# Attention and MLP on one Trainium2 core: transposing k and q on VectorE in 32 by 32 blocks, from block loads on two queues

## The chip, the cores and the metric

The kernel runs on 1 core of one Trainium2 chip. The metric is the device time of one execution in microseconds (us). Four compute engines appear below by short names: PE (TensorE, with its weight loads shown apart as PEld), DVE (VectorE), ACT (ScalarE) and POOL (GpSimd). SP (SyncE) does no arithmetic and issues DMAs; ACT can issue them too. In the profile, SPq and ACTq are the instruction queues of those engines when they issue a DMA.

## The reference

A decayed linear attention over 4 batches, 8 heads, 768 tokens and head size 64, in blocks of 64 tokens, followed by a two-layer MLP on the 3072 x 512 result. Everything is float32.

```python
for b in range(nb):
    sl = slice(b * block, (b + 1) * block)
    qb, kb, vb = (q[:, :, sl], k[:, :, sl], v[:, :, sl])
    intra = np.einsum('bhic,bhjc->bhij', qb, kb) * Dmask[None]
    intra = np.einsum('bhij,bhjd->bhid', intra, vb)
    inter = np.einsum('bhid,bhde->bhie', qb * lam_pow[None], kv_state)
    out[:, :, sl] = intra + inter
    kb_dec = kb * rev_pow[None]
    kv_state = lam_block[None, :, None, None] * kv_state + np.einsum('bhsd,bhse->bhde', kb_dec, vb)
...
h = x @ w_in                      # x: attention output, (3072, 512); w_in: (512, 2048)
g = np.maximum(0.01 * h, h)
return (g @ w_out).astype(np.float32)
```

`Dmask`, `lam_pow`, `rev_pow` and `lam_block` are powers of one factor per head.

## The kernel before

**Tiling.** Tokens come in 24 chunks of 128 (two blocks of 64), six per batch. Four chunks make a group of 512 tokens, so there are six groups. The inner layer is cut into 8 pieces `p` of 256 columns. Each operand of the MLP is kept as three arrays `h`, `l` and `m` (a high part, a scaled rest and a combination), and each product is the sum of three matmul passes over them: `h` and `l` first, then an ACT pass over the PSUM bank (L579), then `m`, and a second ACT pass with the leaky ReLU (L582).

**Stages.** `alone(c)` and `begun(c)` do the first chunks. `round_of(c)` is one attention round: it finishes chunk `c` (`outputs`), forms the scores of chunk `c + 1` (`scores`) and transposes k and q of chunk `c + 2` (`transposes`), and it loads k, q and v of chunk `c + 2`. `up(g, p)` is one up-projection step of a group, 48 matmuls of 512 columns for a whole group (L561), and writes the 512 KB result `G` to DRAM (L585). From group 2 on, every second up step has a round beside it: rounds 12 to 23 stand beside the up steps of groups 2 to 4. When all groups are through, `down_load` and `down` read `G` back and do the second layer (L620) to the end. `w_in(p)` and `w_out(p)` turn the weights, which arrive as 64-bit words, into float32 (three ACT passes, L497 to L501, and two DVE passes, L503 and L504, per half piece); `w_out` then parks its result in DRAM (`WO`, L538), and `w_out_parts` fetches it back in group 5, where the attention buffers are free.

**Transposes.** The scores need k and q with the head dimension on the partitions. `transposes` (L319) does that with four 128 x 128 PE transposes for k into `po` (or a `b` bank for the first chunks) and four for q into `pt` (L331), and two ACT copies bring them into `kTs` and `qTs` (L340, L341). POOL then scales k (L345) and q (L349). k is also needed untransposed, for the state update (`kv`, L364).

**Loads.** `load_kq` (L304) loads k and q of a chunk with two 128 KB DMAs each, all on SP, into the double buffers `kqv[0]` and `kqv[1]`; `load_v` loads v. Rows of 64 floats make packets of 256 bytes.

**Order of the work.** [...] `Plan.add` (L61) records each operation with its engine, an assumed duration, the keys that it reads and writes and a rank; `Plan.emit` (L81) places them by a greedy list schedule and emits the instructions in that order, so every engine's queue is fixed at build time. The plan has one lane called DMA, which stands for SP's queue, and takes a DMA's result as usable 3.5 us after the lane is through with it. In a round, PE's pieces are chained so that nothing comes between them (`plan.begin`, `plan.end`). A small copy `seen_po` (L414) lets PE start the second state product (`inter(1)`, L417); it may go to DVE or ACT, as the plan finds.

**DMA completion.** In the built program all DMAs of SP and ACT share eight landing counters, handed out in turn. A DMA waits for the one that used its counter last, and its issuing engine waits with it, in order.

**Buffers.** `raw` is three buffers of 4 KB per partition for the arriving weight words, used in turn; from the down stage on the last one holds the output scratch `tt`. `gs` is two output buffers of `up`. The PSUM banks `b10`, `b11` and `b2` rotate among the blocks of `up`.

Of the kernel before, what the change touches and what calls it, by code (L numbers as in the profile page):

```python
# [36 lines left out]
class Plan:  # L37
# [23 lines left out]
    def add(self, eng, us, fn, reads=(), writes=(), rank=0.0):  # L61

        n, deps = len(self.ops), set()
        for k in reads:
            w, r = self.last.setdefault(k, [None, []])
            if w is not None:
                deps.add(w)
            r.append(n)
        for k in writes:
            w, r = self.last.setdefault(k, [None, []])  # L70
            if w is not None:
                deps.add(w)
            deps.update(r)
            self.last[k] = [n, []]
        deps.discard(n)
        ways = {eng: us} if isinstance(eng, str) else dict(zip(eng, us))
        if self.chain is not None:
            self.chains[self.chain].append(n)
        self.ops.append((ways, fn, deps, (self.rank + rank, n), set(writes)))
# [81 lines left out]
def kernel(  # L161
# [10 lines left out]
    nc = tc.nc  # L172
    P = 128
    B, H, SEQ, D = q.shape
    C, C2 = P, P // 2
    NCB = SEQ // C
    HP = H // 2
    d_model, d_ff = moe_w_in.shape
    KO = d_model // P
    NP = d_ff // (2 * P)  # L180
    NCH = B * NCB
    GC = 4
    NG = NCH // GC
    T = GC * C
# [3 lines left out]
    QS = 0  # L188
    KM = 1
    NRAW = 3  # L190
    HALF = (slice(0, D), slice(D, 2 * D))
    assert D == 64 and KO == HP == 4 and SEQ % C == 0 and NCH % GC == 0 and d_model == T == 512 and NP % 4 == 0

    pool = ctx.enter_context(tc.tile_pool(name="sb", bufs=1))
    psum = ctx.enter_context(tc.tile_pool(name="ps", bufs=1, space=bass.MemoryType.PSUM))
# [6 lines left out]
    def ps(shape, name):  # L202
        return psum.tile(shape, F32, name=name, tag=name)


    pt = ps([P, HP, C], "pt")
# [6 lines left out]
    X = [[sb([P, KO, T], f"x{x}{i}", F32R) for x in "hlm"] for i in range(2)]  # L213
    raw = [sb([P, 2 * d_model], f"raw{i}") for i in range(NRAW)]
    lows = [sb([P, d_model], f"low{i}", I32) for i in range(2)]
# [11 lines left out]
    def part(n):  # L227
        nonlocal used
        used += n
        assert used <= NA, used  # L230
        return att[:, used - n:used]

    ident = part(P)
    kqv = [[part(H * D).rearrange("p (h d) -> p h d", h=H) for _ in range(2)] for _ in range(3)]
    kTs, qTs, qsTs = ([part(HP * C).rearrange("p (y t) -> p y t", y=HP) for _ in range(2)] for _ in range(3))
    sc = part(2 * HP * C2).rearrange("p (x y t) -> p x y t", x=2, y=HP)
    state = [part(HP * D).rearrange("p (y d) -> p y d", y=HP) for _ in range(4)]
# [21 lines left out]
    add = plan.add  # L259
# [10 lines left out]
    def factors_q():  # L270
        for i in range(2):
            nc.vector.tensor_copy(lam_p[HALF[i]], lam_h[HALF[i], i::2])
        for hp in range(HP):
# [25 lines left out]
    def of(c):  # L299
        return c // NCB, c % NCB, c % 2  # L300
# [3 lines left out]
    def load_kq(c):  # L304
        b, n, i = of(c)
        for src, x, nm in ((k, 0, "k"), (q, 1, "q")):
            y, dst = src[b, :, n * C:(n + 1) * C, :], kqv[x][i]

            def go(y=y, dst=dst):
                for z in range(2):  # L310
                    nc.sync.dma_start(out=dst[:, z * HP:(z + 1) * HP, :], in_=y[z::2].rearrange("h p d -> p h d"))  # L311
            add("DMA", 1.15, go, [], [f"{nm}{i}"])

    def load_v(c):
        b, n, i = of(c)
# [3 lines left out]
    def transposes(c):  # L319
        b, n, i = of(c)  # L320
        tk, tq = kqv[0][i], kqv[1][i]
        if c < GC:
            z, key = bank[KT].rearrange("p (y t) -> p y t", y=HP), KT
            at = [z[:, y, :] for y in range(HP)]
        else:
            z, key = po[:, :, upper, :], "po"
            at = [po[:, y // 2, HP + y % 2 * 2:HP + y % 2 * 2 + 2, :].rearrange("p a t -> p (a t)") for y in range(HP)]

        def go(src, at):
            for y in range(HP):  # L330
                nc.tensor.transpose(out=at[y], in_=src[:, 2 * y:2 * y + 2, :].rearrange("p a d -> p (a d)"), identity=ident)  # L331

        add("PE", 0.44, lambda: go(tk, at), [f"k{i}"], [key])
        add("PE", 0.44, lambda: go(tq, [pt[:, y, :] for y in range(HP)]), [f"q{i}"], ["pt"])

        def copies():
            kT = kTs[i]
            into = kT if c < GC else kT.rearrange("p (t a) x -> p t (a x)", t=2)
            src = z if c < GC else z.rearrange("p t a x -> p t (a x)")
            add("ACT", 0.6, lambda: nc.scalar.copy(into, src), [key], [f"kT{i}"])  # L340
            add("ACT", 0.6, lambda: nc.scalar.copy(qTs[i], pt), ["pt"], [f"qT{i}"])  # L341
            kr = tk.rearrange("p (y x) d -> p y x d", x=2)
            nr = slice(0, C2 if n == NCB - 1 else P)
            add(*((("DVE", "POOL"), (0.7, 1.1)) if c < KM else ("POOL", 1.1)),
                lambda e="POOL": ENG[e].tensor_tensor(kr[nr], kr[nr], _bc(pow_k, 3, D)[nr], op=ALU.mult), ["fk"], [f"k{i}"])  # L345
            m = slice(1 if n == 0 else 0, 2)
            o, x = (z.rearrange("p y (t i) -> p y t i", t=2)[:, :, m, :] for z in (qsTs[i], pt if c < QS else qTs[i]))
            eng, e, us, dep = ("DVE", nc.vector, 0.7, "pt") if c < QS else ("POOL", nc.gpsimd, 1.2, f"qT{i}")
            add(eng, us, lambda: e.tensor_tensor(o, x, _bc(pow_q, 2, 2)[:, :, m, :], op=ALU.mult), ["fq", dep], [f"qsT{i}"])  # L349

        return copies
# [101 lines left out]
    def round_of(c):  # L453

        after = []
        if c + 2 < NCH:
            load_kq(c + 2)
        plan.begin(c)

        if c < 2 * GC:  # L460
            after.append(transposes(c + 2))
        after.insert(0, outputs(c, lambda: after.append(scores(c + 1)) if c + 1 < NCH else None))
        if 2 * GC <= c < NCH - 2:
            after.append(transposes(c + 2))
        plan.end()
        for x in after:
            x()
        if c + 2 < NCH:
            load_v(c + 2)

# [2 lines left out]
    n_raw = 0  # L473

    def to_float32(kind, p, h, dst, key, after=()):

        nonlocal n_raw
        j, n_raw = n_raw % len(raw), n_raw + 1
        r, low, kl = raw[j], lows[n_raw % 2], f"low{n_raw % 2}"
        d = dst.bitcast(I32)  # L480

        def load():
            r64 = r.bitcast(I64)
            if kind == "wi":
                nc.scalar.dma_start(out=r64.rearrange("p (k f) -> p k f", k=2),
                                  in_=w_in_r[:, 2 * h:2 * h + 2, p * 2 * P:(p + 1) * 2 * P])
            else:
                nc.sync.dma_start(out=r64, in_=moe_w_out[(2 * p + h) * P:(2 * p + h + 1) * P, :])

        def words(i, dt):  # L490
            return r.bitcast(dt).rearrange("p (n two) -> p n two", two=2)[:, :, i]

        def addend(dt, i):
            return low.bitcast(dt).rearrange("p (n two) -> p n two", two=2)[:, :, i]

        add("DMA", 1.6, load, after, [f"raw{j}"])
        add("ACT", 0.67, lambda: nc.scalar.activation(out=dst, in_=words(1, F32), func=AF.Abs, scale=2.0 ** -110),  # L497
            [f"raw{j}"], [key])
        add("ACT", 0.78, lambda: nc.scalar.activation(out=addend(U16, 0), in_=words(0, U32), func=AF.Copy, bias=0.0, scale=2.0 ** -29),
            [f"raw{j}"], [kl])  # L500
        add("ACT", 0.77, lambda: nc.scalar.activation(out=addend(F16, 1), in_=words(1, F32), func=AF.Copy, bias=0.0, scale=2.0 ** -100),  # L501
            [f"raw{j}"], [kl])
        add("DVE", 0.42, lambda: nc.vector.tensor_scalar(d, d, 3, None, op0=ALU.logical_shift_left), [], [key])  # L503
        add("DVE", 1.0, lambda: nc.vector.tensor_tensor(d, d, low, op=ALU.add), [kl], [key])  # L504
# [159 lines left out]
    nxt, n_out = 3 * GC, 0  # L664
    steps = [(g, p) for g in range(2, NG) for p in range(NP)]
    for n, (g, p) in enumerate(steps):
        while nxt < (g + 1) * GC:
            seq.append(("r", nxt))
            nxt += 1
        seq.append(("up", g, p))  # L670
        if nxt < NCH and nxt // GC < g + 2 and n % 2 == 0:
            seq.append(("r", nxt))
            nxt += 1
        if n_out < NP and n % 2 == 1:
            seq.append(("wo", n_out, ["G%d%d" % steps[n - 1]]))
            n_out += 1
        if g == NG - 1:
            seq.append(("wp", p))
# [5 lines left out]
    for n, x in enumerate(seq):  # L684
# [9 lines left out]
        elif x[0] == "wp":  # L694
            if not freed:
                add("DVE", 0.0, lambda: None, [], ATT + [f"gr{j}" for j in range(NR)])
                add("ACT", 0.0, lambda: None, [], [f"raw{j}" for j in range(NRAW)] + ["t0", "t1"])
                freed = True
# [37 lines left out]
```

## Time and profile before

| | |
|---|---|
| median of 3 runs | 625.87 us (625.6 to 626.18) |
| the profiled execution | 626.15 us, its span 623.6 us |
| granted TensorE clock | 1.0 throughout |
| DMA | 103706 packets, 101.51 MB, mean 163 GB/s; 78560 packets under 512 B |
| rounds 12 to 22 | one each 14 us, from 153 to 306 us |
| down stage | from 357 us to the end |

The span runs from the first instruction to the last; the execution's own time is 2.55 us more. Engine busy times are sums over the whole span; where stages differ, the tables by stage count. In the chain of waits each piece is what the next one waited for, followed back from the end. A group line gives operation, tiles, shape and count, then busy us and the mean duration in ns. The line "DMA to landing" is the time from the start of the issuing instruction to the landing of its last byte.

### The profile page before, as it was taken

How to read it: one execution, taken by the hardware profiler on the slowest of the kernel's cores; microseconds unless marked ns; L12 is line 12 of the kernel's file. 1: busy time of each engine (PE TensorE's matmuls, PEld its weight loads, DVE VectorE, ACT ScalarE, POOL GpSimd, SP SyncE). 2: the span in 40 equal slices, each digit the busy share in tenths (PEclk: the TensorE clock that was granted, in tenths of full speed). 3: DMA queues.
4: the chain of work that ended last, by engine and by line, in shares of the span. 5: the costliest groups of instructions: out<-in, count | busy, mean ns of one | idle time of the engine just before them, and what ended most of it. 6: DMA issues, size and time to landing. Idle time of an engine off the chain costs nothing.

```text
span 623.6 us, 13157 instructions
## 1 busy us (share of the span) xinstructions
PE 613.9 (98%) x5578; PEld 513.5 (82%) x5578; DVE 297.9 (48%) x366; ACT 281.2 (45%) x461; POOL 91.7 (15%) x95
## 2 busy tenths in 40 slices
PE   8899999999999999999999999999999999999997
PEld 7688888898888888888788888888888888888885
DVE  4799882400344333333145763735545454535531
ACT  3688875443577766664444722312222222314111
POOL 4852513300332222222000000000000000000000
PEclk9999999999999999999999999999999999999999
DMA  9998844632787778842455762432524333333201
GB/s 201 250 259 259 243 156 136 155 111 91 206 248 253 245 238 259 247 163 87 169 202 189 247 203 72 153 117 82 188 67 135 136 106 131 128 109 118 85 0 67
DMA packets 103706, 101.51 MB, mean 163 GB/s; under 512 B 78560, under 2 KB 80608, under 8 KB 103648
## 3 DMA queue, kind: packets, MB, share of 16 engines
q1 hardware_dynamic: 99152, 92.29, 47.3%
q10 hardware_dynamic: 4496, 8.39, 4.3%
q8 instruction: 43, 0.70, 0.5%
q14 instruction: 15, 0.12, 0.1%
HBM read 65.02 MB, written 35.65 MB: 161 GB/s over the span
## 4 chain that ended last, share of the span: by engine, by line
PE 96%; DMA 2%; SPq 0%; POOL 0%; DVE 0%; ACT 0%; issue 0%; DVEq 0%
PE b L561 43%; PE b L620 17%; PE po L620 11%; PE psc L620 10%; PE po L286 4%; PE pt L620 3%; PE psc L286 3%; PE po L331 2%; PE pt L331 2%; DMA att<-in_q_dram 2%; PE b L253 1%; DMA att<-in_k_dram 1%; SPq L311 0%; PE b L331 0%; POOL att L345 0%
## 5 line engine op out<-in xcount | busy, mean ns | idle before, releaser
L602 ACT ACTIVATE xh<-att 128x1024 fp32r<-128x1024 f32 x48 | 50.9, 1061 | 147.3 <-PE po L620 141.3
L603 DVE SCALAR_TENSOR_TENSOR xl<-att,xh 128x1024 fp32r<-128x1024 f32 x48 | 58.7, 1223 | 99.4 <-ACT xh L602 99.4
L561 PE MATMUL b<-xh,wh 128*128 128x512 f32 (+3 forms) x416 | 105.5, 377 | 0.0
L561 PE MATMUL b<-xl,wl 128*128 128x512 f32 (+3 forms) x416 | 105.4, 376 | 0.0
L561 PE MATMUL b<-xm,wm 128*128 128x512 f32 (+3 forms) x416 | 104.9, 381 | 0.0
L561 PEld LDWEIGHTS b<-xl,wl 128*128 128x128 f32 x416 | 75.5, 188 | 14.7 <-DVE wl L515 0.2
L561 PEld LDWEIGHTS b<-xh,wh 128*128 128x128 f32 x416 | 75.3, 188 | 14.3
L561 PEld LDWEIGHTS b<-xm,wm 128*128 128x128 f32 x416 | 73.5, 188 | 13.2
L579 ACT ACTIVATE b<-b 128x512 f32<-128x512 f32 (+2 forms) x98 | 56.7, 579 | 57.1 <-PE b L561 56.3
L582 ACT ACTIVATE gs<-b 128x512 f32<-128x512 f32 (+2 forms) x98 | 57.8, 590 | 48.7 <-PE b L561 40.2
L375 DVE TENSOR_TENSOR att<-psc,att 128x512 f32<-128x512 f32 x24 | 16.5, 688 | 128.3 <-PE psc L286 128.2
L620 PE MATMUL b<-wl,xl 128*128 128x512 f32 x192 | 74.7, 389 | 0.0
L620 PE MATMUL b<-wh,xh 128*128 128x512 f32 x192 | 74.7, 389 | 0.0
L605 DVE SCALAR_TENSOR_TENSOR xm<-xl,xh 128x1024 fp32r<-128x1024 f32 x48 | 58.8, 1226 | 4.8
L345 POOL TENSOR_TENSOR att<-att 128x512 f32<-128x512 f32 (+1 forms) x24 | 27.6, 1149 | 141.1 <-PE po L331 133.5
L620 PEld LDWEIGHTS b<-wh,xh 128*128 128x128 f32 x192 | 36.1, 188 | 7.5
L620 PEld LDWEIGHTS b<-wl,xl 128*128 128x128 f32 x192 | 36.0, 188 | 7.5
L385 POOL TENSOR_TENSOR att<-att 128x256 f32<-128x256 f32 x40 | 35.6, 889 | 28.7 <-DVE att L382 23.4
L620 PE MATMUL po<-wm,xm 128*128 128x512 f32 (+1 forms) x100 | 37.2, 381 | 0.7 <-ACT raw L642 0.7
L620 PE MATMUL psc<-wh,xh 128*128 128x512 f32 x96 | 37.4, 389 | 0.0
L620 PE MATMUL po<-wl,xl 128*128 128x512 f32 x96 | 37.4, 389 | 0.0
L620 PE MATMUL b<-wm,xm 128*128 128x512 f32 x96 | 37.4, 389 | 0.0
(67 smaller groups left out, 817.1 us busy)
## 6 DMA issues: line engine op xcount, KB each, us to landing
att<-g SPq DMA_DIRECT2D x48, 512.0 KB, 3.2
g<-gs SPq DMA_DIRECT2D x45, 512.0 KB, 2.9
raw<-in_moe_w_in_dram ACTq DMA_DIRECT2D x16, 512.0 KB, 5.0
raw<-in_moe_w_out_dram SPq DMA_DIRECT2D x16, 512.0 KB, 4.3
att<-in_k_dram SPq DMA_DIRECT2D x48, 128.0 KB, 4.0
att<-in_q_dram SPq DMA_DIRECT2D x48, 128.0 KB, 3.7
att<-in_v_dram SPq DMA_DIRECT2D x24, 256.0 KB, 3.9
out_dram<-gs SPq DMA_DIRECT2D x23, 256.0 KB, 2.2
```

The source lines that it names most:

```text
L286: nc.tensor.matmul(dst[HALF[cols]], lhsT=lhsT[HALF[rows]], rhs=rhs[HALF[rows]], start=start, stop=True, skip_group_check=True)
L331: nc.tensor.transpose(out=at[y], in_=src[:, 2 * y:2 * y + 2, :].rearrange("p a d -> p (a d)"), identity=ident)
L345: lambda e="POOL": ENG[e].tensor_tensor(kr[nr], kr[nr], _bc(pow_k, 3, D)[nr], op=ALU.mult), ["fk"], [f"k{i}"])
L375: add("DVE", 0.69, lambda: nc.vector.tensor_tensor(sc, psc[:, :, lower, :], decay, op=ALU.mult), ["psc", "fk"], ["sc"])
L385: add("POOL", 0.7, lambda new=new, j=j: nc.gpsimd.tensor_tensor(state[(j + 1) % 4], new, _bc(lam_c, 2, D), op=ALU.mult), [f"st{j % 4}", "f ...
L561: nc.tensor.matmul(dst, lhsT=w[z][:, kk * 2 * P + f * P:kk * 2 * P + (f + 1) * P], rhs=x[z][:, kk, toks], start=start and kk == 0, stop=kk ...
L579: add("ACT", ns, lambda b=b: nc.scalar.activation(out=b, in_=b, func=AF.Copy, bias=0.0, scale=S + 1.0), [], [kb], rank=-1.5)
L582: add("ACT", ns, lambda b=b, r=r: nc.scalar.activation(out=r, in_=b, func=AF.Prelu, bias=0.0, scale=1.0 / WS, alpha=0.01), [kb], [f"gs{jg} ...
L602: add("ACT", 1.05, lambda: nc.scalar.activation(out=h, in_=graw[j], func=AF.Copy, bias=0.0, scale=NEAR), reads, wr("h"))
L603: add("DVE", 1.25, lambda: nc.vector.scalar_tensor_tensor(l, graw[j], 1.0, h.bitcast(F32), op0=ALU.mult, op1=ALU.subtract), reads + [f"rh{ ...
L605: add("DVE", 1.25, lambda: nc.vector.scalar_tensor_tensor(m, l.bitcast(F32), -S, h.bitcast(F32), op0=ALU.mult, op1=ALU.add), [f"rh{j}", f" ...
L620: nc.tensor.matmul(acc[tb][z // 2][:, cols], lhsT=ring[j][z][:, f * T + tb * P:f * T + (tb + 1) * P], rhs=W[pp][z][:, f * d_model:(f + 1) ...
```

## The change

From chunk 12 on (`DV = 12`) k and q are no longer transposed on PE. VectorE transposes them straight into `kTs` and `qTs`, from SBUF to SBUF, with one instruction for a chunk's k and one for its q (`turn`). Such an instruction transposes each 32 x 32 block in its place and moves no block to other partitions. So the data must arrive with the blocks already where the result wants them: for each pair of chunks, `load_subs` issues 32 DMAs, 16 for k on SP and 16 for q on ACT, each with 32 partitions of 8 runs of 32 floats (32 KB, runs of 128 bytes). k's blocks go into the third `raw` buffer; q's go into the second `raw` buffer for the pair of chunks 12 and 13 and after that into the two q buffers, which are free because the plain q loads end at chunk 12. The plain k loads stay. A pair's loads are recorded in the round four before its first chunk, after the transposes of the chunk three ahead, with a rank 5 later than the rest of that round; each load has its own rank and place in the plan. An issue on ACT is entered with 0.45 us on ACT's lane.

Three things follow. `kqv` is cut from one piece per letter so that the two q buffers lie side by side. The w_out loads use only the first two `raw` buffers. And a w_out piece is converted every third up step instead of every second, so that the last one falls on step 22 rather than on step 15 (of 32).

In the built program TensorE has 96 transposes fewer (12 chunks of eight), ACT 24 copies fewer and 96 DMA issues more, VectorE 24 transposes more, SP 96 issues more and 24 plain q loads fewer; `seen_po` is copied by VectorE in 14 rounds instead of 3.

```diff
@@
+    SUBQ, SUBR, SUBD = ("DMA", "ACT"), 5.0, 0.0
+
+    DV = 12
+    C4 = P // 4
@@
-    kqv = [[part(H * D).rearrange("p (h d) -> p h d", h=H) for _ in range(2)] for _ in range(3)]
+    kqv_f = [part(2 * H * D) for _ in range(3)]
+    kqv = [[x[:, i * H * D:(i + 1) * H * D].rearrange("p (h d) -> p h d", h=H) for i in range(2)] for x in kqv_f]
@@ load_kq
-            add("DMA", 1.15, go, [], [f"{nm}{i}"])
+            if nm == "k" or c < DV:
+                add("DMA", 1.15 if c < DV else 1.5, go, [], [f"{nm}{i}"])
+
+    def subs(c):
+
+        two = ((k, raw[-1], [f"raw{NRAW - 1}"]), (q, raw[-2], [f"raw{NRAW - 2}"]) if c < DV + 2 else (q, kqv_f[1], ["q0", "q1"]))
+        return [(x, y.rearrange("p (y t) -> p y t", y=HP), keys) for x, y, keys in two]
+
+    def load_subs(c):
+        b, n, i = of(c)
+        for nm, eng, (src, sub, keys) in zip("kq", SUBQ, subs(c)):
+            add("DVE", 0.0, lambda: None, [], keys)
+            for y in range(HP):
+                for a in range(4):
+                    h = y // 2 + (2 * y + a // 2) % HP * 2
+                    z = src[b, h, n * C:(n + 2) * C, a % 2 * C4:(a % 2 + 1) * C4]
+                    o = sub[a * C4:(a + 1) * C4, y, :]
+                    add(eng, 0.58 if eng == "DMA" else 0.45,
+                        lambda o=o, z=z, e=nc.sync if eng == "DMA" else nc.scalar: e.dma_start(
+                            out=o.rearrange("j (m i) -> j m i", i=C4), in_=z.rearrange("(m j) i -> j m i", j=C4)),
+                        keys, [f"{nm}s{y}{a}"], rank=SUBR + SUBD * (4 * y + a))
+            add("DMA", 0.0, lambda: None, [f"{nm}s{y}{a}" for y in range(HP) for a in range(4)], [f"{nm}s"])
+
+    def turn(c):
+        i = c % 2
+        for nm, (_, sub, keys), dst in zip("kq", subs(c - i), (kTs[i], qTs[i])):
+            add("DVE", 0.7, lambda a=dst, b=sub: nc.vector.transpose(out=a, in_=b[:, :, i * C:(i + 1) * C]),
+                keys + [f"{nm}s"] + [f"{nm}s{y}{a}" for y in range(HP) for a in range(4)], [f"{nm}T{i}"])
@@ transposes
-        add("PE", 0.44, lambda: go(tk, at), [f"k{i}"], [key])
-        add("PE", 0.44, lambda: go(tq, [pt[:, y, :] for y in range(HP)]), [f"q{i}"], ["pt"])
+        if c < DV:
+            add("PE", 0.44, lambda: go(tk, at), [f"k{i}"], [key])
+            add("PE", 0.44, lambda: go(tq, [pt[:, y, :] for y in range(HP)]), [f"q{i}"], ["pt"])
...
-            add("ACT", 0.6, lambda: nc.scalar.copy(into, src), [key], [f"kT{i}"])
-            add("ACT", 0.6, lambda: nc.scalar.copy(qTs[i], pt), ["pt"], [f"qT{i}"])
+            if c < DV:
+                add("ACT", 0.6, lambda: nc.scalar.copy(into, src), [key], [f"kT{i}"])
+                add("ACT", 0.6, lambda: nc.scalar.copy(qTs[i], pt), ["pt"], [f"qT{i}"])
@@ round_of
         for x in after:
             x()
+        if DV <= c + 3 < NCH:
+            turn(c + 3)
+        if DV <= c + 4 < NCH and c % 2 == 0:
+            load_subs(c + 4)
@@ to_float32
-        j, n_raw = n_raw % len(raw), n_raw + 1
+        j, n_raw = n_raw % (len(raw) - (kind == "wo")), n_raw + 1
@@ the sequence of steps
-        if n_out < NP and n % 2 == 1:
+        if n_out < NP and n % 3 == 1:
```

More of the change, by code (lines that the diff above doesn't have):

```diff
@@ L190 @@
     NRAW = 3
+    SUBQ, SUBR, SUBD = ("DMA", "ACT"), 5.0, 0.0
+    DV = 12
+    C4 = P // 4
     HALF = (slice(0, D), slice(D, 2 * D))
-    assert D == 64 and KO == HP == 4 and SEQ % C == 0 and NCH % GC == 0 and d_model == T == 512 and NP % 4 == 0
+    assert DV % 2 == NCB % 2 == 0 and D == 64 and KO == HP == 4 and SEQ % C == 0 and NCH % GC == 0 and d_model == T == 512 and NP % 4 == 0
     pool = ctx.enter_context(tc.tile_pool(name="sb", bufs=1))
```

## The prediction, made before the change was run

> **What bounds the kernel now.** I read the page's shares first, then the chain of waits between 195 and 310 us, then a table of stages cut at the starts of the attention rounds, and last the landings of the loads that the change imitates.
>
> ```profile
> PE 613.9 (98%) x5578; PEld 513.5 (82%) x5578; DVE 297.9 (48%) x366; ACT 281.2 (45%) x461; POOL 91.7 (15%) x95
> ```
>
> TensorE has 98% of the span, everything else less than half of it except weight loads, which run beside the matmuls. The chain says whether that 98% is a true bound. It is: from 195 to 310 us it is TensorE alone but for 0.2%, and it repeats one round.
>
> ```profile
> 265.01 0.86 PE po L286 x48
> 265.87 0.93 PE psc L286 x64
> 266.80 0.23 PE po L286 x16
> 267.04 0.58 PE po L331 x4
> 267.62 0.44 PE pt L331 x4
> 268.06 10.93 PE b L561 x48
> ...
> 292.96 0.86 PE po L286 x48
> 293.81 0.87 PE psc L286 x44
> 294.68 0.29 PE po L286 x16
> 294.98 11.11 PE b L561 x48
> ```
>
> Columns: start, length, engine and line. The reader should see that a round is attention quads (L286), eight transposes (L331), then 48 up-projection matmuls (L561), and that the round at 292.96, which has no chunk left to transpose, goes without the L331 pieces. The stages put a price on this:
>
> ```profile
> 181.26:195.24 13.98, 13.98 (x189) 11.72 (x192) 5.47 (x9) 9.95 (x18) 4.05 (x4) 1.00 0.79 246
> 278.98:292.96 13.98, 13.98 (x189) 11.73 (x192) 3.69 (x5) 6.34 (x12) 3.51 (x4) 1.00 0.28 96
> 292.96:306.08 13.12, 13.12 (x164) 10.88 (x166) 2.31 (x4) 5.48 (x10) 0.00 (x0) 1.00 0.27 93
> ```
>
> Columns: stage, its length, busy us of PE, PEld, DVE, ACT and POOL, clock, DMA share, GB/s. TensorE fills each stage. A round that also converts w_out (first line) is as long as one that doesn't (second line), though ACT's work differs by 3.6 us: ACT and the DMAs are hidden, with 4.0 us of a round left on ACT in the fullest rounds and the DMA engines 0.79 busy.
>
> [...] The trace of before has no VectorE transpose. [...] a k or q load on SP (L311) takes 0.46 us to issue, but up to 1.7 us where it waits. [...] No run here shows two queues under load yet.
>
> **The change part by part.**
>
> *Transposes off TensorE.* Chunks 12 to 23 are transposed in rounds 10 to 21: 12 rounds lose eight transposes. From above (13.98) and below (13.12) the round without them is 0.86 us shorter; the chain shows 0.58 + 0.44 = 1.02 us, of which 11.11 - 10.93 = 0.18 comes back, because the first matmul after quads starts later than after a transpose. I take 12 x 0.85 = 10.2 us; were the 0.18 not to come back it would be 12.2.
>
> *Their ACT copies.* 24 copies (L340, L341) of about 0.59 us vanish: 1.2 us of ACT per round. Not on the path; it makes room for the next item.
>
> *Block loads.* 32 loads of 32 KB for each pair of chunks, 16 on SP for k and 16 on ACT for q; the plain q loads go (4 per pair) and the plain k loads stay for the state update. How much issuing costs ACT is seen where before issues its w_in loads:
>
> ```profile
> 21.94 0.79 ACT L499 ACTIVATE low<-raw 128x512 uint16<-128x512 uint32 x1
> 22.17 0.39 ACTq L485 DMA_DIRECT2D raw<-in_moe_w_in_dram  x1
> 22.58 0.15 ACT L414 COPY att<-po 128x2 f32<-128x2 f32 x1
> ```
>
> The issue (0.39 us) lies inside the running ACTIVATE, and the next starts 0.64 us after the former one, no later than without. So one issue after an ACTIVATE costs 0 to 0.1 us, a further one straight behind it 0.4. In the new program's ACT stream the 96 issues stand in 49 groups, so some 49 x 0.05 + 47 x 0.4 = 21 us in all, 1.8 us per round over 12 rounds. ACT then has 9.95 - 1.2 + 1.8 = 10.6 us in a round that converts w_out; of 13.1 us that leaves 2.5 us. Hidden, as long as no issue *waits*.
>
> *The waits that come with them.* In the order of the built program every DMA, from either queue, waits until the one eight places before it has landed (the eight landing counters are handed out in turn). Before has 10 DMAs in a round of 14 us, and eight places back is at least 9.7 us ago nine times in ten, so this never shows. After has about 45 in two rounds. Counting the TensorE work that stands between in the program (0.91 us for four 512-column matmuls, 2.19 us for a round's attention), the DMA eight places before an ACT issue lies 4.1 us back in the median, under 3.2 us in 23 of 96. What a load needs to land:
>
> ```profile
> L311 SPq DMA_DIRECT2D att<-in_k_dram x18: 457/514/1707, 154.6 to 266.8; - x18
> ...
> DMA to landing us min/median/max: 2.3/3.6/4.5
> ```
>
> These are 128 KB loads between 153 and 280 us. Packets of 256 B took 18.2 ns and those of 4 KB 181 ns there (packet records of the trace), so 512 packets over 16 engines are 0.58 us of the 3.6. A block load has 256 packets of 128 B. [...] With the other DMAs of a burst (2.9 for G, 4.3 for w_out) the mean is about 3.25. A burst of n DMAs through eight places takes n/8 of that. The six bursts hold 37, 35, 39, 40, 40 and 38 DMAs and are spread in the program over 15.6, 12.1, 21.1, 18.9, 20.2 and 17.1 us of TensorE work. Only the second is too dense: 35/8 x 3.25 = 14.2, 2.1 over. TensorE rides over about 1 us, since between a block's l matmuls and its m matmuls stand the other block's (1.82 us), of which ACT's L579 uses 0.59. That leaves 1.1 us of stall, and I add 0.2 for local crowding in each of the other five: 2.1 us, with 0 and 5.6 as ends (the latter from a landing of 3.7, below).
>
> What is behind a waiting issue: on ACT the L579 and L582 evictions, which free TensorE's banks, and the w_out conversions; on SP the G writes (two gs buffers, their reuse some 7 us later in program order), the k and v loads and the w_out loads. The latter land 1.6 to 4.8 us before ACT takes them today, so a delay up to 1.6 us costs nothing; a longer one stops ACT itself.
>
> *VectorE.* 24 transposes of 128 x 512 fp32. [...] a 512-column tensor_tensor (L375) took 0.69. I take 0.7, with 0.55 and 1.4: two per round, 1.4 us. DVE has 5.5 of 13.98 busy, so 7 us remain, and it stood idle 8.24 us before L375 in the round at 195. At 1.4 each it would still be hidden. The turn waits for 16 landings; behind it in DVE's order stand L375 and the small copy L414 (which moves to DVE in 11 more rounds), on which TensorE's second state product waits. That copy stands 5 us or more of TensorE work behind the turn in most rounds.
>
> *w_out every third step.* Same 16 loads and conversions, now up to round 23 rather than 19: 3.6 us of ACT per round become 2.4 on average. The last ends two steps before its parts are wanted. 0 us; it eases ACT and DMA. [...]
>
> *Sum.* Profiled execution 626.15 us (span 623.6): 626.15 - 10.2 + 2.1 = 618.05. It lies 0.28 over the median 625.87, so **617.8 us**.
>
> **The rivals.** *A, the forecast:* 615.3 to 620. *B, half given back:* landings average 3.7 us because the DMA engines are fuller. The same sums give 0.5 and 3.1 us of stall in the first two bursts, and 2 us for crowding: 5.6, so 621.3. For it: w_out loads took 4.3. Against: block loads are short, and half go round SP's long ones. *C, slower:* the eight places become the bound, at ACT's DMA issues in rounds 8 to 19. ACT stands in front of a landing while L579 waits behind, TensorE runs out of banks, and the whole round stretches. By the same sums, less 1 us of cover each, the gain is gone from a mean landing of 4.2 us (2.8 + 5.3 + 1.1 + 1.9 = 11.1). At 4.5 it is 4.2 + 6.6 + 2.6 + 1.3 + 3.3 = 18.0, so 633.7. For it: single loads of before took 4.5 and w_out's 5.4, and DMA share rises. Against: the median is 3.6 for four times the bytes. *D, nothing:* DVE's turn waits so long that L414 costs each round what the transposes did; two such errors would have to match.
>
> **How the numbers follow.** A 0.52, B 0.20, C 0.24, D 0.04. A measurement of this kernel tells 0.2% (1.25 us) from no change; A and B are faster, C slower, so 0.72, 0.04, 0.24. The range runs from 615.3 (A without stall) to 628, past B and into the mild part of C, and leaves out most of C.
>
> **What would show it.** Right: rounds 13.1 us long, no L331 from chunk 12 on, L579 and L582 released by PE and not late, ACT issues near 0.4 us. Wrong: ACT issues of 1 us and more with TensorE gaps behind L579 or L582 (B or C), landings over 4 us, gaps before the second L286 po group released by DVE (D), or VectorE transposes over 1.4 us.

## The result, and the profile after

| | before | after |
|---|---|---|
| median | 626.18 us (20 runs, 625.59 to 630.48) | 622.89 us (20 runs, 620.14 to 626.99) |
| ratio after / before | | 0.9948, 95% interval 0.993 to 0.9965 |
| the profiled execution | 626.15 us | 623.09 us, its span 621.3 us |
| TensorE's stalls between 90 and 330 us, in sum | 0.3 us | 4.3 us |

The change makes the kernel 3.3 us faster. The forecast was 8.1 us (617.8 against 625.87), so the direction was right and the size less than half. Stalls are counted here and below from the starts of TensorE's matmuls: each start that comes more than 0.13 us later than the usual pace counts with all that it is late. The 4.3 us are the one gap of 0.27 us that before has too, and 4.0 us in five new places. What TensorE waited for there stands in its waits (who waited for whom: us, times, longest; waits under 0.15 us are left out):

```profile
PE po L291 <- DVE att L448: 3.0, 3, 2.2
PE b L599 <- ACT b L617: 0.8, 2, 0.5
```

The new program has other line numbers. L599 are the matmuls of `up`, L617 and L620 the two ACT passes over a PSUM bank, L623 the write of `G`, L291 the attention quads, L448 the `seen_po` copy, L526 the w_out loads, L535 to L539 their conversion on ACT and L541 and L542 on VectorE, L335 the block loads and L343 the VectorE transposes.

First the windows of the new profile, for three rounds (stage, length, busy us of PE, PEld, DVE, ACT and POOL, clock, DMA share, GB/s).

```profile
168.15:181.28 13.13, 13.13 (x180) 10.89 (x182) 5.55 (x10) 8.87 (x15) 2.92 (x3) 1.00 0.81 218
181.28:194.42 13.14, 13.14 (x181) 10.90 (x183) 5.83 (x12) 6.82 (x12) 4.53 (x5) 1.00 0.91 251
...
232.00:245.00 13.00, 10.81 (x150) 8.83 (x150) 6.41 (x12) 7.81 (x15) 3.08 (x3) 1.00 0.78 200
```

A quiet round is 13.13 us long instead of 13.98: the 0.85 us per round came as forecast. In the third stage TensorE is busy for only 10.8 of 13 us. Its longest gap, 2.18 us, ends at 238.69; the timeline of ACT leads there. A square bracket gives the idle time before an instruction and its releaser.

```profile
228.43 0.60 ACT L620 ACTIVATE gs<-b 128x512 f32<-128x512 f32 x1 [0.62 <-PE b L599]
228.45 0.32 ACTq L335 DMA_DIRECT2D att<-in_q_dram  x1
229.29 0.58 ACT L617 ACTIVATE b<-b 128x512 f32<-128x512 f32 x1 [0.26 <-PE b L599]
229.29 2.27 ACTq L335 DMA_DIRECT2D att<-in_q_dram  x3
231.62 0.58 ACT L617 ACTIVATE b<-b 128x512 f32<-128x512 f32 x1 [1.74 <-DMA g<-gs]
234.30 0.32 ACTq L335 DMA_DIRECT2D att<-in_q_dram  x1
234.72 0.60 ACT L620 ACTIVATE gs<-b 128x512 f32<-128x512 f32 x1 [2.52 <-PE b L599]
236.49 0.37 ACTq L335 DMA_DIRECT2D att<-in_q_dram  x1
236.96 0.60 ACT L620 ACTIVATE gs<-b 128x512 f32<-128x512 f32 x1 [1.64 <-PE psc L291]
237.45 0.65 ACT L535 ACTIVATE w<-raw 128x512 f32<-128x512 f32 x1
```

Read the ACTq lines against the holes between the ACT lines: before 234.72 and before 236.96 there stands a block-load issue. The bracket names PE as the releaser, but PE had long been done; ACT stood at the issue. What the issue waited for is found from the landing counters of the trace:

| issued by | what | issue | landing | counter |
|---|---|---|---|---|
| SP | G write, 512 KB | 227.83 | 231.23 | 101 |
| SP | w_out, 512 KB | 228.22 | 234.28 | 103 |
| ACT | q block | 228.45 | 236.13 | 105 |
| SP | w_out, 512 KB | 228.72 | 235.97 | 106 |
| ACT | q block | 229.29 | 236.47 | 107 |
| SP | k block | 229.56 | 236.30 | 100 |
| ACT | q block | 229.66 | 236.64 | 108 |
| ACT | q block | 231.25 | 236.80 | 101 |
| SP | k block | 231.46 | 236.97 | 102 |
| ACT | q block | 234.30 | 237.13 | 103 |
| SP | k block | 236.15 | 239.13 | 105 |
| ACT | q block | 236.49 | 239.29 | 107 |

Three of ACT's issues come 0.02 us after the landing that had their counter before: 231.25 after 231.23, 234.30 after the w_out load's 234.28, 236.49 after 236.47. This is the window of eight, at work: in the whole trace none of ACT's 96 block-load issues starts before that landing, and 23 start 0.02 us after it. Behind the second and third of the three the w_out conversion L535 came late, and VectorE with it:

```profile
238.14 0.43 DVE L541 TENSOR_SCALAR w<-w 128x512 int32<-128x512 int32 x1 [15.27 <-ACT w L535]
238.48 0.15 DVE L448 COPY att<-po 128x2 f32<-128x2 f32 x1
```

VectorE had nothing to do for 15 us but stood at L541. The little copy L448 that TensorE needed was next in line, and TensorE went on at 238.69.

The chain of waits takes another branch here, through SP's queue, but it shows how long one of these loads was under way (start, length, what):

```profile
228.43 0.03 ACT gs L620
228.45 7.68 DMA att<-in_q_dram
236.13 0.02 issue
236.15 0.31 SPq L335
236.46 0.04 issue
236.50 2.02 SPq L335
```

A 32 KB load took 7.7 us, and SP's next block load stood until its counter came free. (TensorE's gap hung on its neighbour, the load of 229.29, which took 7.2 us and had the counter that ACT's issue of 236.49 needed.) The table shows what was under way beside them: a G write and two w_out loads of 512 KB each, on SP. The four block loads issued between 228.4 and 229.7, three of them on ACT's own queue, landed between 236.1 and 236.7: behind the large ones, not around them. One of the four was issued even before the second w_out load.

### The profile page after: what moved, and what is told of

The parts are those of the page before. It is cut to its first block, busy times and chain, and to the rows that moved or that the text cites. A ratio compares the mean times of both kernels' runs of the same rounds, so it can differ in the third digit from the quotient of the medians.

```text
span 621.3 us, 13134 instructions
## 1 busy us (share of the span) xinstructions
PE 606.5 (98%) x5482; PEld 504.4 (81%) x5482; DVE 306.9 (49%) x401; ACT 266.8 (43%) x426; POOL 90.9 (15%) x95
## 4 chain that ended last, share of the span: by engine, by line
PE 87%; DMA 8%; ACT 2%; DVE 1%; SPq 1%; issue 1%; POOL 0%; DVEq 0%; ACTq 0%
PE b L599 37%; PE b L658 18%; PE po L658 11%; PE psc L658 11%; DMA att<-in_q_dram 4%; PE pt L658 3%; PE po L291 3%; PE psc L291 3%; DMA att<-in_v_dram 2%; DMA att<-in_k_dram 1%; DMA raw<-in_moe_w_out_dram 1%; PE pt L363 1%; SPq L335 1%; ACT low L537 1%; PE b L258 1%
## 5 line engine op out<-in xcount | busy, mean ns | idle before, releaser
L599 PE MATMUL b<-xh,wh 128*128 128x512 f32 (+3 forms) x416 | 105.8, 377 | 0.0
L599 PE MATMUL b<-xm,wm 128*128 128x512 f32 (+3 forms) x416 | 104.6, 382 | 0.8 <-ACT b L617 0.8
L599 PE MATMUL b<-xl,wl 128*128 128x512 f32 (+3 forms) x416 | 105.2, 376 | 0.0
L599 PEld LDWEIGHTS b<-xl,wl 128*128 128x128 f32 x416 | 75.5, 188 | 14.5
L599 PEld LDWEIGHTS b<-xh,wh 128*128 128x128 f32 x416 | 75.0, 188 | 14.2
L599 PEld LDWEIGHTS b<-xm,wm 128*128 128x128 f32 x416 | 73.3, 188 | 16.2 <-ACT b L617 2.3
L620 ACT ACTIVATE gs<-b 128x512 f32<-128x512 f32 (+2 forms) x98 | 57.7, 589 | 54.7 <-PE b L599 46.9
L617 ACT ACTIVATE b<-b 128x512 f32<-128x512 f32 (+2 forms) x98 | 55.8, 576 | 59.1 <-PE b L599 47.2
L383 POOL TENSOR_TENSOR att<-att 128x512 f32<-128x512 f32 (+1 forms) x24 | 30.3, 1263 | 83.9 <-PE po L291 31.1
L419 POOL TENSOR_TENSOR att<-att 128x256 f32<-128x256 f32 x40 | 33.7, 843 | 38.5 <-DVE att L416 35.0
L658 PE MATMUL pt<-wm,xm 128*128 128x512 f32 x96 | 37.3, 389 | 0.0
```

Source lines behind the costliest of these rows:

```text
L419: add("POOL", 0.7, lambda new=new, j=j: nc.gpsimd.tensor_tensor(state[(j + 1) % 4], new, _bc(lam_c, 2, D), op=ALU.mult), [f"st{j % 4}", "f ...
L599: nc.tensor.matmul(dst, lhsT=w[z][:, kk * 2 * P + f * P:kk * 2 * P + (f + 1) * P], rhs=x[z][:, kk, toks], start=start and kk == 0, stop=kk ...
L617: add("ACT", ns, lambda b=b: nc.scalar.activation(out=b, in_=b, func=AF.Copy, bias=0.0, scale=S + 1.0), [], [kb], rank=-1.5)
L620: add("ACT", ns, lambda b=b, r=r: nc.scalar.activation(out=r, in_=b, func=AF.Prelu, bias=0.0, scale=1.0 / WS, alpha=0.01), [kb], [f"gs{jg} ...
L658: nc.tensor.matmul(acc[tb][z // 2][:, cols], lhsT=ring[j][z][:, f * T + tb * P:f * T + (tb + 1) * P], rhs=W[pp][z][:, f * d_model:(f + 1) ...
```

## The experiments

Theory 1: small block loads land late and hold ACT through the eight shared counters. Its variants: 1b, the eight are short whichever engine issues; 1c, the large transfers keep the DMA engines busy, whatever counters they use. Theory 2: the seen_po copy is late because of VectorE's own queue. Theory 3: the loss lies in the first 40 us and is not the change's.

All were timed beside the kernel before. Stalls are counted as above, in the profile between 90 and 330 us and without the 0.27 us that before has too; a stretch of slow matmuls counts with what it lost.

| kernel | median us | ratio to before | stalls us |
|---|---|---|---|
| the changed kernel | 622.89 | 0.9948 (0.993 to 0.9965) | 4.0 |
| two plain loads | 617.1 | 0.9858 (0.9842 to 0.9874) | 0.6 |
| all on SP | 635.19 | 1.0139 (1.0115 to 1.0163) | 17.1 |
| no w_out loads | 618.71 | 0.9877 (0.9863 to 0.9892) | 2.1 |
| seen_po on ACT | 625.03 | 0.9976 (0.9962 to 0.999) | 7.3 |
| w_out halves apart | 624.01 | 0.9957 (0.9943 to 0.997) | 6.4 |
| w_out every second step | 633.37 | 1.0115 (1.0093 to 1.0138) | 18.3 |
| w_out part alone | 626.51 | 1.0006 (0.9994 to 1.0018) | 0 |
| q from GpSimd | 619.14 | 0.9883 (0.9865 to 0.9901) | 1.8 |
| w_out from GpSimd | 628.85 | 1.0041 (1.0028 to 1.0054) | 10.1 |
| q from GpSimd, seen_po on ACT | 617.06 | 0.9848 (0.983 to 0.9866) | 0.5 |
| q from GpSimd, w_out every second step | 623.52 | 0.9944 (0.9921 to 0.9967) | 4.3 |
| changed, again | 623.36 | 0.9949 (0.9934 to 0.9963) | 7.6 |

In all but four the instructions are emitted in the order of the changed kernel, and only a queue, an engine or a load is exchanged. The four are those that move w_out's steps; "w_out part alone" starts from the kernel before.

**Two plain loads.** Each letter's 16 block loads become one load of the same 512 KB in plain rows, without the block order.

```diff
-  e.dma_start(out=o.rearrange("j (m i) -> j m i", i=C4), in_=z.rearrange("(m j) i -> j m i", j=C4))
+  w.append(e.dma_start(out=o, in_=z[0:P * 8 * P].rearrange("(p x) -> p x", p=P))) if not w else None
```

> Leaves out the block order of the data: each letter's 16 block loads of 32 KB are replaced by one plain 512 KB load of q or k in 4 KB rows, issued where the first of the 16 stood; the order of all other instructions is the changed kernel's, the turns read other numbers. It shows what the change is worth without its many small DMAs. Theory 1 (the small loads wait for the eight landing counters and hold ACT): 616 to 618, a ratio to before of 0.983 to 0.988, TensorE gaps after 30 us under 1 us in sum. Theory 2 (the seen_po copy, now on VectorE, is late for reasons of VectorE's own queue): 620 to 622, with the gaps released by L448 still there. Theory 3 (the loss is in the first 40 us and has nothing to do with the loads): 622 to 623.

Measured 617.1. With the same TensorE work and the same VectorE transposes, 5.8 us of the changed kernel's time hang on the many small loads. The gap at 238 is gone though L448 is still on VectorE, and what is left (0.55 us near 314) is the new end of the up stage. So theory 2 falls as a cause by itself, and theory 3 as the main one. Part of theory 3 holds for the first profile: compared matmul by matmul with this kernel, which runs the same matmuls, it is 1.4 us behind by 90 us, where the block loads begin. In the second profile of the changed kernel (below) that is 0.2 us.

**No w_out loads.**

```diff
-  nc.sync.dma_start(out=r64, in_=moe_w_out[...])
+  pass
```

> Leaves out the sixteen 512 KB w_out loads (their conversions run on old data); all else in the same order. Theory 1 with the large loads as the trigger (block loads that follow them land 5 to 8 us after issue): 619 to 620.5, the gaps near 219 and 239 us gone, block loads landing under 3.5 us everywhere. Theory 1 without them (32 small loads are too many for eight counters by themselves): 622 to 623. Theory 2: 622 to 623. Theory 3: 622 to 623.

Measured 618.71: 4.2 us come back when the large loads go, and the gaps at 219 and 239 with them. Not all was as expected: ACT still waits for block loads, as its waits between 90 and 320 us say (who waited for whom: us, times, longest):

```profile
ACT gs L620 <- DMA att<-in_q_dram: 8.7, 6, 3.1
ACT b L617 <- DMA att<-in_q_dram: 6.1, 4, 1.8
ACT xh L464 <- DMA att<-in_q_dram: 4.2, 2, 3.1
```

With 2.7 us at the first pair's loads these are 22 us. That is as much as in the changed kernel, where the waits name block loads for 17 us and the three brackets before 231.62, 234.72 and 236.96 above add 5.9 us under other names; yet TensorE's stalls are only 2.1 us. Nor do all block loads land under 3.5 us: the longest of ACT's took 5.3. In this run waits of up to 3.1 us were mostly ridden over; in the changed kernel the gap of 2.18 us stood behind two in a row, of 2.52 and 1.64 us.

**All on SP.** ACT issues none of the block loads.

```diff
-  e=nc.sync if eng == "DMA" else nc.scalar
+  e=nc.sync
```

> Same order, but q's block loads are issued by SP too, so ACT never waits for a landing. Theory 1, if ACT's waiting is what costs: 618 to 620 (ratio 0.988 to 0.991), no gap released by ACT or by a VectorE step that waited for ACT. Theory 1b (the eight counters are short whoever issues): SP's G writes, k, v and w_out loads are late in their turn, 622 to 627. Theory 2: 622 to 623, as the changed kernel. Theory 3: 622 to 623.

Measured 635.19, outside what theory 1 gave and past the end of 1b. ACT doesn't wait for block loads now, but for what SP brings late:

```profile
ACT w L535 <- DMA raw<-in_moe_w_out_dram: 15.4, 6, 5.7
ACT gs L620 <- DMA g<-gs: 14.0, 6, 3.6
```

L620 waits because the G write that frees its `gs` buffer stands behind block loads in SP's queue. Taking the wait from ACT is no remedy if it goes to another queue that TensorE depends on.

**seen_po on ACT.**

```diff
-  lambda e: (nc.vector.tensor_copy if e == "DVE" else nc.scalar.copy)(seen_po, ...)
+  lambda e: nc.scalar.copy(seen_po, ...)
```

> Same order, but the seen_po copy is always done by ACT (before it was in 21 of 24 rounds; in the changed kernel in 10). Theory 2 (VectorE's queue is the fault): the gaps released by L448 (0.50 and 2.18 us) go, 619.5 to 620.5. Theory 1 (ACT is the late one; the copy then stands behind ACT's issues instead): gaps of the same sum or more, now released by ACT, 622 to 625. Theory 3: 622 to 623.

Measured 625.03, at the upper end of what theory 1 gave: the gaps stay (1.19 us at 219.5, 2.28 at 239.5, a new 0.95 at 262.5), now released by ACT's copy. ACT was the late one; VectorE only passed it on.

**The spacing of w_out.** Three kernels: halves on different steps (`w_out` then does one half at a call), every second step as before, and the w_out part of the change alone on the kernel before.

```diff
-  if n_out < NP and n % 3 == 1:
-      seq.append(("wo", n_out, ["G%d%d" % steps[n - 1]]))
+  if n_out < 2 * NP and n % 3 > 0:                                   # halves apart
+      seq.append(("wo", n_out // 2, n_out % 2, ["G%d%d" % steps[n - 1]]))
...
-  if n_out < NP and n % 3 == 1:
+  if n_out < NP and n % 2 == 1:                                      # every second step
```

> The changed kernel with the two 512 KB loads of a w_out piece on different up steps (n % 3 = 1 and 2) instead of together. Theory 1 with the large loads as the trigger: the longest backlog in front of a block load halves (7.7 us landings become 4 to 5), gaps released by L448 and L617 between 100 and 320 us fall from 4.0 us to 1 to 2, 619.5 to 621. If the large loads hurt singly as much as in pairs (16 of them instead of 8 times 2): 622 to 624.

> The changed kernel with the w_out pieces back at every second up step, as before (still two raw buffers). Theory 1 with the large loads as the trigger: pieces fall into more of the bursts (steps 1 to 15, with block loads until about step 16), so 623.5 to 626, more gaps than 4.0 us. If the every-third-step spacing was worth nothing: 622 to 623.5.

> The kernel before with only the w_out part of the change: every third step, two raw buffers. All theories: 625.5 to 626.5, no change against before (ratio 0.999 to 1.001), since nothing waits for w_out there. If the spacing or the lost buffer had a cost of its own: 627 and more.

Halves apart: 624.01, no better. The plan came out in another order, with ACT's issues closer together. The block loads that ACT issued from 195 to 207 us land 1.7 to 4.1 us after their issue, none over 5, and ACT is nevertheless held, once for 4.3 us, because so many stand in a row; TensorE loses 1.3 and 2.9 us there. So this run doesn't say whether singles hurt less than pairs.

Every second step: 633.37, more than expected. The same spacing on the kernel before is worth nothing (ratio 1.0006, the interval includes 1); inside the change it is worth 10.5 us. It was not a side edit, but what keeps the change, with its loads on ACT, from being a loss.

**q from GpSimd.** GpSimd's DMAs have eight landing counters of their own in the built program (111 to 118), and it stood at 15% busy.

```diff
-  e=nc.sync if eng == "DMA" else nc.scalar
+  e=nc.sync if eng == "DMA" else nc.gpsimd
```

> Same order as the changed kernel, but q's block loads are issued by GpSimd, whose DMAs have eight landing counters of their own; ACT issues none, SP has its eight for itself. Theory 1 (sharing of eight counters, ACT's waits): 617.5 to 620, no gap released by ACT or by a VectorE step behind ACT. Theory 1c (the DMA engines are full behind the w_out loads, whoever issues; the turn and the k loads are late anyway): 622 to 624. A cost of GpSimd's own issue (its k and q scalings L379 and L383 come behind the loads and the scores wait): 623 to 635 with gaps before the psc or po quads released by POOL.

Measured 619.14: 3.8 us better than the changed kernel. Three things come with the exchange. SP has its eight counters to itself. GpSimd's queue moves a block load in 16 packets of 2 KB instead of 256 of 128 B, with 16 of 4 B behind them in either case (the queue's line: packets, MB, share of 16 engines). And an issue occupies GpSimd for 0.59 us:

```profile
q0 software_dynamic: 3072, 3.15, 2.2%
...
L335 POOL DMA_DIRECT2D att<-in_q_dram x80 | 46.5, 589 | 1.6 <-DVE att L343 0.8
```

The DMAs themselves did *not* get faster. From the landings in the trace, 110 to 270 us:

| from issue to landing, us | changed | no w_out loads | q from GpSimd | changed, again |
|---|---|---|---|---|
| q block loads: median, mean, longest | 3.0, 3.33, 7.7 | 2.6, 2.73, 5.3 | 3.4, 3.93, 7.2 | 3.1, 3.36, 7.9 |
| of 80, over 5 us | 10 | 1 | 21 | 9 |
| w_out loads: mean | 5.8 | none | 6.2 | 6.1 |
| all DMAs: mean | 3.34 | 2.97 | 3.88 | 3.45 |

Loads land *later* in the faster kernel. What changed is who stands in front of them. ACT's release and SP's relief come together in this run, which can't tell them apart.

**w_out from GpSimd.** The large loads leave the eight shared counters, the small ones stay.

```diff
-  nc.sync.dma_start(out=r64, in_=moe_w_out[...])
+  nc.gpsimd.dma_start(out=r64, in_=moe_w_out[...])
```

> Same order as the changed kernel; only the sixteen w_out loads are issued by GpSimd, so they occupy none of the eight counters that SP and ACT share[...]; the block loads stay on SP and ACT. Theory 1 in the form 'the counters' (a slow large load at the counter eight places back holds ACT and SP): 618.5 to 620.5, near the kernel without w_out loads (618.7). Theory 1c, 'the DMA engines' (small loads land late because the large ones are being moved, whatever counter they have): 622 to 624, gaps behind the w_out loads as in the changed kernel.

Measured 628.85: worse than the changed kernel, so taking the large loads out of the shared counters is no remedy, and "the large loads occupy the counters" falls as the cause. ACT's timeline at the worst gap (4.55 us, to 211.08):

```profile
200.00 0.58 ACT L617 ACTIVATE b<-b 128x512 f32<-128x512 f32 x1 [0.26 <-PE b L599]
200.01 7.39 ACTq L335 DMA_DIRECT2D att<-in_q_dram  x5
207.50 0.60 ACT L620 ACTIVATE gs<-b 128x512 f32<-128x512 f32 x1 [6.91 <-DMA att<-in_q_dram]
207.52 2.88 ACTq L335 DMA_DIRECT2D att<-in_q_dram  x4
210.45 1.07 ACT L617 ACTIVATE b<-b 128x512 f32<-128x512 f32 x2 [2.35 <-DMA att<-in_q_dram]
```

GpSimd issued two w_out loads at 198.87 and 199.46, which landed at 204.67 and 206.38. ACT's block loads of 200.01, 200.37 and 201.59 landed at 206.73, 207.07 and 207.49. Three queues, and the small loads still landed 0.35 to 1.11 us after the second of the large ones, 5.9 to 6.7 us after their own issue. So in this run the delay came without counters in common with the large loads; the window of eight turned it into a hold of the engine that issues next, 7.39 us for ACT's five issues from 200.01. The exchange moved the large loads too: the two that go out at 206.06 and 207.27 in the changed kernel go out at 198.87 and 199.46 here, in the middle of a burst. That may be why this kernel is worse and not just no better; no run shows it.

**The two fixes together, and the hard case.** With ACT no longer held, its copy should be on time; and the dense w_out spacing should hurt less.

```diff
+  e=nc.sync if eng == "DMA" else nc.gpsimd          # both
+  lambda e: nc.scalar.copy(seen_po, ...)             # the first
+  if n_out < NP and n % 2 == 1:                      # the second
```

> q's block loads from GpSimd, and the seen_po copy always on ACT. With ACT no longer held, the copy should be on time there: the two gaps left (0.63 and 0.67 us, released by VectorE's copy) go, 617.5 to 618.5. If ACT's own work (evictions, w_out conversions) makes it late: 619 to 621, with gaps released by ACT L448.

> q's block loads from GpSimd with the w_out pieces at every second up step, which costs 10.5 us (633.4 against 622.9) where ACT issues q's loads. Theory 1 (counters and ACT's waits): most of that goes, 619 to 622. Theory 1c (DMA engines full): 628 to 633.

The first, 617.06, is the fastest kernel of the study: 1.5% under before, and level with the one that has no small loads at all (617.1). The copy that gained nothing on ACT in the changed kernel is right there once ACT doesn't wait. ACT's waits between 150 and 310 us have no block load of q left:

```profile
ACT gs L620 <- PE b L599: 29.1, 45, 2.2
ACT b L617 <- PE b L599: 27.7, 33, 1.2
ACT att L448 <- PE po L291: 5.4, 9, 1.6
```

The second, 623.52, is 9.9 us better than the same spacing with ACT as the issuer, but 4.4 us worse than with every third step. Of the 10.5 us that the dense spacing costs with ACT as the issuer, 6.1 are gone and 4.4 stay, so 619 to 622 was missed. ACT waits for no block load here. The longest gap left, 1.74 us to 256.73, ends with an L617 that stood behind six conversion passes of ACT in a row (251.72 to 255.60).

**The changed kernel again**, unedited, for a second profile.

> The changed kernel once more, unedited, for a second profile. Theory 1 in its refined form (small loads land behind whatever large transfers are already handed to the DMA engines, and the engine that has eight outstanding is held): the gaps between 100 and 320 us are again released by ACT L617 or by VectorE's L448 behind ACT, 3 to 7 us in sum, with block loads of 5 us and more from ACT just before them; 621.5 to 624.5. Theory 3 (a start that happened to be bad): a profile with less lost in the first 40 us is nearer 620.5, and the gaps later are under 2 us.

Measured 623.36. The gap at 238.5 is there again, 2.87 us, released by L448 behind ACT: the place belongs to the program, not to a chance. And something follows it (windows, columns as above):

```profile
230.00:235.00 5.00, 5.00 (x95) 4.03 (x97) 0.00 (x0) 0.58 (x1) 0.00 (x0) 1.00 0.87 243
235.00:240.00 5.00, 2.12 (x50) 1.77 (x43) 2.03 (x5) 3.81 (x7) 0.15 (x1) 0.80 0.61 159
240.00:245.00 5.00, 5.00 (x13) 3.85 (x13) 3.60 (x6) 2.61 (x5) 3.04 (x3) 0.52 0.88 243
245.00:250.00 5.00, 5.00 (x24) 4.12 (x23) 2.64 (x5) 2.38 (x4) 1.64 (x2) 1.00 0.27 111
```

In 240 to 245 TensorE is busy all the time, but with 13 matmuls where the window after has 24, and the granted clock is 0.52. The matmuls start 427 ns apart instead of 228. About 2.75 us are lost in this way, nearly as much again as the gap itself.

## Why the prediction was right in direction and wrong in size

- *TensorE's own gain.* Forecast 12 x 0.85 = 10.2 us. Shown: rounds of 13.13 us. The kernel with two plain loads gains 9.1, after giving back 0.55 us in a gap near 314 us that wasn't foreseen; the other 0.5 us is open.
- *VectorE.* Forecast 0.7 us per transpose, hidden. Measured 681 and 689 ns, the instruction's line and mean being:

```profile
L343 DVE STREAM_TRANSPOSE att<-raw 128x512 f32<-128x512 f32 x14 | 9.2, 681 | 0.0
```

- *Packets.* A packet of 128 B took 12.7 ns on average in the trace (110 to 270 us). The forecast's landing near 3.2 us for a block load was the author's estimate, which no trace of before shows: it has no load of 32 KB. The measured medians are 3.0 us for q's on ACT and 2.6 for k's on SP.
- *The failed step: the window of eight counters.* This is the term of 2.1 us, and it measures 5.8 (622.89 against 617.1). The forecast took a mean landing of 3.25 us, compared it with the mean spacing of each burst, and put 1.1 us on the second burst, the only one too dense, and 0.2 us on each of the others. The mean was right (3.34). The place was not. Matmul by matmul against the kernel with two plain loads, the six bursts cost 0.8, 0.3, 0, 0, 3.3 and 0.3 us in the first profile, and 0.8, 0.8, 0, 0, 6.6 and 0.3 in the second, slow matmuls included. The fifth is the one at 228 us, with a G write and two w_out loads between its block loads. What held the queue here was not the mean, but landings that were long together: ten of ACT's 80 loads took over 5 us, in three bunches beside the w_out loads of the fourth, fifth and sixth burst. What stands behind the wait decides as well, since only the bunch of the fifth cost much. And crowding alone did it in one run: with halves apart the mean is 2.9 us, only two loads took over 5, and 6.4 us of stall remain. How the loss is shared among these isn't settled. "Block loads are short, and half go round SP's long ones", the argument against rival B, is what the table of landings above and the run with w_out from GpSimd contradict.
- *What stands behind.* The forecast named evictions and w_out conversions behind a waiting issue, and the seen_po copy behind the turn. It didn't join the two: the copy stood behind L541, L541 behind ACT's conversion, and that behind ACT's issue.
- *The w_out spacing.* "0 us; it eases ACT and DMA." Alone it is 0; with the block loads it is worth 10.5 us. An edit that costs nothing by itself was the one that set the sign.
- *The clock.* Not in the forecast at all. Averaged over the runs the granted clock was 0.998 before and 0.996 after; 0.002 of 621 us is 1.2 us. In the second profile it dropped at the gap of 2.87 us (0.80 in 235 to 240 us, 0.52 in 240 to 245). In the first, the only slow stretch before the end, at 0.5, runs from 22.16 to 25.57, before any block load. How much of the 1.2 us comes from the one and how much from the first 40 us, where either program can lose a microsecond or two while it waits for its first loads, isn't settled.
- *The sum.* Forecast -10.2 + 2.1 = -8.1. Measured -9.1 (without the small loads) + 5.8 (with them) = -3.3, where the 5.8 holds what the clock and the first 40 us add. In the two profiled executions, changed and two plain loads, the last matmul comes 6.0 us later: 1.4 us before 90 us and 4.6 us in the bursts. The stalls of the table, counted another way, differ by 3.4 us. The lower end of the forecast's range, 615.3, doesn't follow from its sum, which gives 615.7 without stall.
- *The rivals.* B gave nearly the measured time (621.3), with 5.6 us of stall; but its reason, a mean landing of 3.7 us, is not what happened, and q from GpSimd has a mean of 3.88 and only 1.8 us of stall. That its number is near is luck. C's mechanism, ACT in front of a landing with TensorE behind it, is the one that was seen, only mild. With w_out every second step the kernel is slower, as in C; that 633.4 lies so near C's 633.7 is luck, since C's figure was for another kernel. D did not happen.

## What to carry to other kernels

Before many small DMAs are put beside large ones, ask for each issuing engine what TensorE work stands behind its queue, and let the engine with the most slack issue them; whether the DMAs get faster matters less (with q from GpSimd the mean landing of the q loads rose from 3.33 to 3.93 us, while the kernel went from 622.89 to 619.14). Judge the wait by the largest landings that come together and by how closely the issues stand, not by the mean, and look at what large transfer was handed over just before. An edit that is free alone should be tried inside the change and without it: spacing the large loads was worth nothing before and 10.5 us after.

## What the runs showed of the hardware that was not expected

- 32 KB loads issued on one queue 0.55 and 0.91 us after a 512 KB load on another landed 0.35 and 0.69 us after it, 6.7 us after their own issue (w_out from GpSimd, 200.01 and 200.37). In the changed kernel the packet records show where such a time goes: the first packet of ACT's four block loads of 228.45 to 231.25 ran only 3.40 to 4.73 us after the issue, where those of 225.13 to 227.33 needed 0.95 to 1.18 us (packets given to loads in the order of issue on their queue). From 233.5 to 234.5 us 51 packets of 4 KB and 203 of 128 B from SP's queue and 354 of 128 B from ACT's ran in the same stretch. The number of packets alone doesn't decide it: GpSimd's block loads, with 16 packets of data each, took 5.8 to 6.8 us where they went out beside large loads (q from GpSimd, 226.62 to 229.49). What holds the first packet back isn't shown.
- Half the clock came with some gaps of TensorE and not with others. In the second profile of the changed kernel a granted clock of 0.52 (240 to 245 us; matmuls 427 ns apart against 228) came with a gap of 2.87 us. In the first, 3.41 us at 0.5 (from 22.16) followed one of 1.72 us, which ended at 20.56, while after the one of 2.18 us, which ended at 238.69, the clock stayed at 1.00. So the second profile lost 2.87 us in its gap at 238.5 and about 2.75 more behind it, the first 2.18 us in all, and the length of the gap alone didn't tell which.
